# A retention, expert and rational-FFN kernel on one core: reordering the last stage's first steps, a drain, the y copies and the last two blocks

## The chip, the cores and the metric

The kernel runs on one core of a Trainium2 chip. The metric is the device time of one execution in microseconds (us). The engines have queues of their own and run in program order, each instruction waiting on semaphores for what it needs: TensorE (PE; its weight loads PEld overlap its matmuls), VectorE (DVE), ScalarE (ACT), GpSimd (POOL) and SyncE (SP), which issues most of the DMAs.

## The reference

Three stages follow one another. The change lies in the third, and touches the end of the second.

```python
# 1: a linear recurrence per head gives 1536 rows of 512 (B*S = 1536, D = 512)
state = gamma * state + k_t v_t^T;   y_t = scale * q_t @ state
# 2: each row goes to its best of 8 experts
h = relu(disp @ w1);   y = h @ w2;   x[i] = gate_w[i] * y[expert_idx[i], pos[i]]
# 3: a feed-forward layer with a rational function between two products
h = x @ w_in                                  # 512 -> 2048
P = a[0] + a[1] * h + a[2] * h*h + a[3] * h*h*h
Q = 1.0 + abs(b[0]) * abs(h) + abs(b[1]) * h*h
out = (P / (Q + 1e-06)) @ w_out               # 2048 -> 512
```

## The kernel before

The order of the work on each engine is the order in which the code issues it; no scheduler moves anything. Every product is made of three matmuls: an operand is split into a rounded part and the rest (`hi`, `lo`), and hi*hi, hi*lo and lo*hi are added up in a PSUM bank.

**The end of stage two.** Expert e has 256 rows in two tiles m = 0, 1. Its second product ends in two banks, which ScalarE copies out with the gate as scale (`y`, line 885); POOL then scatters the 128 rows of `y` to the DRAM table `yd` (line 787). The rows lie there sorted by expert, so the last two of the twelve tiles of 128 rows, 10 and 11, are loaded (`y_load`, `yr<-yd`) behind the scatters of the last expert. `y_tile` (lines 952 to 967) transposes a tile on TensorE into a bank (`ytp`) and splits it: ScalarE writes `yh`, VectorE `yl`.

**Stage three.** Four tiles of rows are one group `tb` of 512 rows (three groups), and the 2048 hidden columns are 16 chunks of 128. A chunk for one group is a *block*; there are 48, n = 0 to 47, and `ffn_at` gives each its quarter q of the weights, its group and its chunk f. Four blocks in a row add into the same four output banks `o` (one for each tile of the group), which are then drained into `acc`. The steps of a block:

- `ffn_a`: 12 matmuls give h (128 x 512) in a bank of its own (`l1`; four banks in turn, so block n+4 takes the bank of block n).
- `ffn_i`: three ScalarE passes (x, |h| and w; lines 995 to 997).
- `ffn_p`: two VectorE passes on x (lines 1004, 1005), and a POOL product for Q (line 1006).
- `ffn_r`: Ln and Exp on ScalarE (lines 1011, 1012); the result is 1/Q, written over h in its bank.
- `ffn_e`: three VectorE passes (lines 1017 to 1019): a Newton step, and P/Q into x. After them the bank of h is free.
- `ffn_g`: ScalarE rounds x to `gh` (line 1029), POOL makes the rest `gl` (line 1031; VectorE for the last two blocks).
- `ffn_b`: 12 matmuls, three for each tile m, add to the banks `o[m]`.

Step n of `ffn_step` issues a(n) and the later steps of older blocks: r(n-2), e(n-3), g(n-4), b(n-5) (`LAG`). Steps 0 to 3 stand between the last expert's second product, steps 4 to 52 in the loop of `ffn`. The eight banks are in four kinds (`BANKS`): `tp` (0, 1) takes transposes and the outputs o[0], o[1]; `l2` (2, 3) takes the experts' second product, the transposes of tiles 10 and 11, and o[2], o[3]; `l1` (4 to 7) takes h.

The first drain is that of block 3, in step 8 (`early`): before the change it is issued ahead of e(5) and p(7). Block 46 has no `ffn_b` of its own; block 47 does both. A finished tile of the output is scattered by POOL (`put_out`, line 1079).

Of the kernel before, what the change touches and what calls it, by code (L numbers as in the profile page):

```python
# [34 lines left out]
NA = 48  # L35
# [38 lines left out]
class Build:  # L74
# [742 lines left out]
    def moe(self):  # L817
        nc = self.nc
        with ExitStack() as st:
            self.dp = self.pool("dec", stack=st)  # L820
            self.mp = self.pool("moe", stack=st)
            self.outs = {}
            self.el, self.gx, self.gg, self.acc, self.pair = {}, {}, {}, {}, {}
            mp = self.mp
            self.xh, self.xl = {}, {}
            self.first_expert()
            for e in range(1, E):
# [4 lines left out]
                for fp in range(4):  # L832
                    i = 4 * e + fp // 2
                    wh, wl = self.whi[i], self.wlo[i]
                    ps = self.bank("l1").rearrange("p (a n) -> p a n", a=2)
# [27 lines left out]
                for hf in range(2):  # L863
                    i = 4 * e + 2 + hf
                    wh, wl = self.whi[i], self.wlo[i]
                    for m in range(2):
                        ms = slice(m * 128, m * 128 + 128)
                        for fl in range(4):
                            f = hf * 4 + fl
                            fh, fo = hh[f // 2][:, f % 2, ms], hl[f // 2][:, f % 2, ms]  # L870
                            ws = slice(fl * 512, fl * 512 + 512)
# [126 lines left out]
        self.el[n] = (x, w, h2, h)  # L998

    def ffn_p(self, n):  # L1000
        nc = self.nc
        ab = self.ab
        x, w, h2, h = self.el[n]
        nc.vector.tensor_tensor(out=x, in0=x, in1=h, op=ALU.mult)
        nc.vector.scalar_tensor_tensor(out=x, in0=x, scalar=ab[:, 1:2], in1=h, op0=ALU.add, op1=ALU.mult)
        nc.gpsimd.tensor_tensor(out=w, in0=h2, in1=w, op=ALU.mult)  # L1006
# [30 lines left out]
    def ffn_b(self, n):  # L1037
        first = n % 4 == 0 and (n == 0 or self.ffn_at(n - 1)[1] != self.ffn_at(n)[1])
        if first:
            self.ob = self.out_banks()  # L1040
        if n == 46:
            return
        ns = (46, 47) if n == 47 else (n,)
        gs = [self.gg.pop(k) for k in ns]
        for m in range(4):
            ps = self.ob[m]
            ms = slice(m * 128, m * 128 + 128)
            for k, (gh, gl) in zip(ns, gs):
                q, tb, f = self.ffn_at(k)
                last = f == 3 and (k == 47 or self.ffn_at(k + 1)[1] != tb)  # L1050
                wh, wl = self.whi[33 + 2 * q], self.wlo[33 + 2 * q]
                ws = slice(f * 512, f * 512 + 512)
                self.nc.tensor.matmul(ps, lhsT=gh[:, ms], rhs=wh[:, ws], start=first, stop=False)  # L1053
                self.nc.tensor.matmul(ps, lhsT=gh[:, ms], rhs=wl[:, ws], start=False, stop=False)  # L1054
                self.nc.tensor.matmul(ps, lhsT=gl[:, ms], rhs=wh[:, ws], start=False, stop=last)  # L1055
            if last:
                self.ffn_out(n, q, tb * 4 + m, ps)

# [30 lines left out]
    def ffn(self):  # L1089
        with ExitStack() as st:  # L1090
# [3 lines left out]
            for n in range(4, NA + LAG[3]):  # L1094
                self.ffn_step(n)

    def ffn_step(self, n):
        lr, le, lg, lb = LAG
        if n < NA:
            self.ffn_a(n)  # L1100
        if 0 <= n - lg < NA:
            self.ffn_g(n - lg)
        if 0 <= n - lr < NA:
            self.ffn_r(n - lr)
        if n < NA:
            self.ffn_i(n)
        early = n == lb + 3
        if early:
            self.ffn_b(n - lb)
        if 0 <= n - le < NA:  # L1110
            self.ffn_e(n - le)
        if 0 <= n - 1 < NA:
            self.ffn_p(n - 1)
        if n == 4:
            self.y_tile(8, self.bank("tp", "ytp"))
            self.y_tile(9, self.bank("tp", "ytp"))
        if n == 5:
            self.y_tile(10, self.bank("l2", "ytp"))
            self.y_tile(11, self.bank("l2", "ytp"))
        if n >= lb and not early:  # L1120
            self.ffn_b(n - lb)
            for t in self.outs.pop(n - 1, ()):
                self.put_out(t)
        if n in LOAD_AT:
            self.load_w(*LOAD_AT[n])
        for k in DEC_AT.get(n, ()):
            self.dec_act(k)
            self.dec_direct(k)
        for i, h in SPLIT_AT.get(n, ()):
            self.split_w(i, h)  # L1130
# [108 lines left out]
```

## Time and profile before

| | |
|---|---|
| time, median of 3 runs (lowest to highest) | 563.97 us (561.2 to 570.03) |
| the profiled execution: time | 562.63 us |
| its span, first to last instruction | 560.9 us |
| TensorE's mean granted clock | 0.994 of full |
| TensorE busy | 542.4 us, 97% of the span |
| DVE, ACT, POOL busy | 408.9, 391.2, 277.3 us |

The time of an execution is its span and some 1.7 us around it. In the tables of the trace, times are microseconds from the start of the span; an arrow names what ended the idle time of the engine ahead of an instruction.

### The profile page before, as it was taken

Reading aid. Unit: us, or ns where it says so; the run is one execution under the profiler, and the core shown is the slowest. Engines: PE = TensorE matmul, PEld = TensorE weight load, DVE = VectorE, ACT = ScalarE, POOL = GpSimd, SP = SyncE. Lnnn points to the kernel's source line nnn. Section 1 sums busy time; section 2 is a strip of 40 time slices with the busy share of each in tenths; the row PEclk is TensorE's granted clock in tenths of the full one; section 3 lists DMA queues with packets and bytes.
Section 4 is the critical chain, followed back from the end, with each engine's and each line's share of the span. In section 5 each row is a group of like instructions: output and inputs, shape, how many; then the busy total and the mean of one; then the engine's idle time right before and its main releaser. Section 6 shows DMA issues by size and latency. Waiting matters only on the chain.

```text
span 560.9 us, 9964 instructions
## 1 busy us (share of the span) xinstructions
PE 542.4 (97%) x3755; PEld 454.0 (81%) x3755; DVE 408.9 (73%) x627; ACT 391.2 (70%) x609; POOL 277.3 (49%) x212
## 2 busy tenths in 40 slices
PE   8999999999999999999997899999999999999994
PEld 4888887897898988989886788878787888888882
DVE  3537757576967768687548387889898999865972
ACT  2677853765666756666586789899979997766750
POOL 5545312308557373222053354667656766545673
PEclk9999999999999999999998999999999999999998
DMA  8689745497799999995323000222222200000212
GB/s 292 250 310 350 247 153 187 143 348 252 248 306 396 291 336 261 374 348 200 113 98 121 1 0 1 76 76 75 76 70 79 78 0 2 0 1 1 77 44 106
DMA packets 31171, 89.54 MB, mean 160 GB/s; under 512 B 6350, under 2 KB 6606, under 8 KB 31120
## 3 DMA queue, kind: packets, MB, share of 16 engines
q1 hardware_dynamic: 27216, 78.38, 41.8%
q0 software_dynamic: 3904, 10.50, 5.2%
q8 instruction: 30, 0.49, 0.4%
q14 instruction: 21, 0.17, 0.1%
HBM read 75.22 MB, written 14.69 MB: 160 GB/s over the span
## 4 chain that ended last, share of the span: by engine, by line
PE 64%; ACT 4%; DVE 3%; issue 2%; POOL 2%; POOLq 0%; ACTq 0%; DVEq 0%
PE h L982 7%; PE h L984 7%; PE h L983 7%; PE o L1053 6%; PE o L1055 6%; PE o L1054 6%; PE l L840 4%; PE l L842 4%; PE l L841 4%; PE l L874 4%; PE l L873 4%; PE l L872 4%; DVE wlo L137 1%; POOL out L1079 1%; PE tp L810 1%
## 5 line engine op out<-in xcount | busy, mean ns | idle before, releaser
L137 DVE TENSOR_TENSOR wlo<-raw,whi 128x1024 fp32r<-128x1024 f32 x80 | 107.6, 1354 | 25.6 <-ACT whi L131 24.8
L1031 POOL TENSOR_TENSOR gg<-fx,gg 128x512 fp32r<-128x512 f32 x46 | 65.8, 1432 | 69.6 <-issue 54.4
L131 ACT ACTIVATE whi<-raw 128x1024 fp32r<-128x1024 f32 x80 | 83.7, 1054 | 4.2 <-PE l L874 4.0
L1053 PE MATMUL o<-whi,gg 128*128 128x512 f32 x192 | 75.8, 395 | 4.0 <-DVE yl L965 3.1
L982 PE MATMUL h<-yh,whi 128*128 128x512 f32 x192 | 76.6, 399 | 2.4 <-DVE fx L1019 2.4
L984 PE MATMUL h<-yh,wlo 128*128 128x512 f32 x192 | 75.7, 394 | 0.0
L1055 PE MATMUL o<-whi,gg 128*128 128x512 f32 x192 | 75.5, 393 | 0.0
L983 PE MATMUL h<-yl,whi 128*128 128x512 f32 x192 | 75.5, 393 | 0.0
L1054 PE MATMUL o<-wlo,gg 128*128 128x512 f32 x192 | 74.9, 390 | 0.0
L995 ACT ACTIVATE fx<-h,ab 128x512 f32<-128x512 f32 x48 | 37.3, 777 | 47.2 <-PE h L984 47.1
L1006 POOL TENSOR_TENSOR fw<-fh,fw 128x512 f32<-128x512 f32 x48 | 62.4, 1299 | 9.7 <-ACT fw L997 9.6
L840 PE MATMUL l<-xh,whi 128*128 128x256 f32 x224 | 63.6, 284 | 1.1 <-DVEq L895 1.1
L842 PE MATMUL l<-xh,wlo 128*128 128x256 f32 x224 | 62.6, 279 | 0.0
L841 PE MATMUL l<-xl,whi 128*128 128x256 f32 x224 | 62.5, 279 | 0.0
L193 POOL TENSOR_TENSOR dw<-gq 128x512 int32<-128x512 int32 x16 | 23.1, 1443 | 62.1 <-DVE gq L190 33.6
L1053 PEld LDWEIGHTS o<-whi,gg 128*128 128x128 f32 x192 | 36.0, 188 | 12.7 <-DVE yl L965 3.8
L982 PEld LDWEIGHTS h<-yh,whi 128*128 128x128 f32 x192 | 36.5, 190 | 11.9 <-DVE fx L1019 4.1
L872 PE MATMUL l<-whi,hh 128*128 128x512 f32 x112 | 45.0, 402 | 0.0
L874 PE MATMUL l<-whi,hl 128*128 128x512 f32 x112 | 44.2, 395 | 0.0
L873 PE MATMUL l<-wlo,hh 128*128 128x512 f32 x112 | 44.2, 394 | 0.0
L1017 DVE SCALAR_TENSOR_TENSOR fw<-fw,cq,h 128x512 f32<-128x512 f32 x48 | 35.6, 741 | 11.4 <-ACT h L1012 11.4
L840 PEld LDWEIGHTS l<-xh,whi 128*128 128x128 f32 x224 | 42.0, 188 | 1.8 <-ACT y L885 1.6
(163 smaller groups left out, 1295.7 us busy)
## 6 DMA issues: line engine op xcount, KB each, us to landing
raw<-wm SPq DMA_DIRECT2D x64, 512.0 KB
r<-wf SPq DMA_DIRECT2D x32, 512.0 KB
vq<-vq SPq DMA_DIRECT2D x11, 512.0 KB
kk<-kk SPq DMA_DIRECT2D x11, 512.0 KB
wd<-dw SPq DMA_DIRECT2D x16, 256.0 KB
raw<-wd SPq DMA_DIRECT2D x8, 512.0 KB
xd<-xs SPq DMA_DIRECT2D x12, 256.0 KB
yr<-yd SPq DMA_DIRECT2D x12, 256.0 KB
```

The lines of the kernel that those rows point to most:

```text
L131: nc.scalar.activation(out=self.whi[i][:, sl], in_=raw, func=AF.Copy)
L137: nc.vector.tensor_tensor(out=self.wlo[i][:, sl], in0=raw, in1=self.whi[i][:, sl].bitcast(F32), op=ALU.subtract)
L840: nc.tensor.matmul(ps[:, fi], lhsT=wh[:, sl], rhs=xh[:, k], start=(k == 0), stop=False)
L841: nc.tensor.matmul(ps[:, fi], lhsT=wh[:, sl], rhs=xl[:, k], start=False, stop=False)
L842: nc.tensor.matmul(ps[:, fi], lhsT=wl[:, sl], rhs=xh[:, k], start=False, stop=(k == 3))
L872: nc.tensor.matmul(acc[m], lhsT=fh, rhs=wh[:, ws], start=(f == 0), stop=False)
L982: nc.tensor.matmul(h, lhsT=wh[:, sl], rhs=yh[:, k], start=(k == 0), stop=False)
L983: nc.tensor.matmul(h, lhsT=wh[:, sl], rhs=yl[:, k], start=False, stop=False)
L984: nc.tensor.matmul(h, lhsT=wl[:, sl], rhs=yh[:, k], start=False, stop=(k == 3))
L1053: self.nc.tensor.matmul(ps, lhsT=gh[:, ms], rhs=wh[:, ws], start=first, stop=False)
L1054: self.nc.tensor.matmul(ps, lhsT=gh[:, ms], rhs=wl[:, ws], start=False, stop=False)
L1055: self.nc.tensor.matmul(ps, lhsT=gl[:, ms], rhs=wh[:, ws], start=False, stop=last)
```

## The change

In steps 0 to 4, a flag `soon` issues g, r and e of a block one step earlier, p at the head of the step, and r behind i rather than ahead of it. The y copies of tiles 8 to 11 stand ahead of ffn_i in steps 4 and 5, no more behind ffn_p. The drain of block 3 in step 8 stands at the end of the step, behind e(5) and p(7), as in every other step. The matmuls of blocks 46 and 47 are interleaved by another list.

```diff
 def ffn_b(self, n):
...
-        ns = (46, 47) if n == 47 else (n,)
-        gs = [self.gg.pop(k) for k in ns]
-        for m in range(4):
-            ps = self.ob[m]
-            ms = slice(m * 128, m * 128 + 128)
-            for k, (gh, gl) in zip(ns, gs):
...
+        order = [(n, m) for m in range(4)]
+        if n == 47:
+            order = [(46, 0), (46, 1), (47, 0), (46, 2), (47, 1), (46, 3), (47, 2), (47, 3)]
+        gs = {k: self.gg.pop(k) for k in sorted({k for k, _ in order})}
+        for k, m in order:
...
+    def ffn_do(self, kind):
+        step, ns = self.todo[kind]
+        for n in ns:
+            step(n)
+
     def ffn_step(self, n):
         lr, le, lg, lb = LAG
+        soon = 1 if n < 5 else 0
+        for kind, lag, step in (("g", lg, self.ffn_g), ("r", lr, self.ffn_r), ("e", le, self.ffn_e)):
+            hi = min(NA, n - lag + soon + 1)
+            self.todo[kind] = (step, range(self.upto.get(kind, 0), hi))
+            self.upto[kind] = max(hi, self.upto.get(kind, 0))
         if n < NA:
             self.ffn_a(n)
-        if 0 <= n - lg < NA:
-            self.ffn_g(n - lg)
-        if 0 <= n - lr < NA:
-            self.ffn_r(n - lr)
+        if soon:
+            self.ffn_p(n - 1)
+        self.ffn_do("g")
+        if not soon:
+            self.ffn_do("r")
+        for t in {4: (8, 9), 5: (10, 11)}.get(n, ()):
+            self.y_tile(t, self.bank("tp" if n == 4 else "l2", "ytp"))
         if n < NA:
             self.ffn_i(n)
-        early = n == lb + 3
-        if early:
-            self.ffn_b(n - lb)
-        if 0 <= n - le < NA:
-            self.ffn_e(n - le)
-        if 0 <= n - 1 < NA:
+        if soon:
+            self.ffn_do("r")
+        self.ffn_do("e")
+        if not soon:
             self.ffn_p(n - 1)
-        if n == 4:
-            self.y_tile(8, self.bank("tp", "ytp"))
-            self.y_tile(9, self.bank("tp", "ytp"))
-        if n == 5:
-            self.y_tile(10, self.bank("l2", "ytp"))
-            self.y_tile(11, self.bank("l2", "ytp"))
-        if n >= lb and not early:
+        if n >= lb:
             self.ffn_b(n - lb)
```

The number and kind of the instructions are the same on every engine. POOL and SP keep their order, and TensorE's differs only in the last 24 matmuls.

ScalarE in steps 4 and 5, before (`fx`, the first `fh` and `fw` are i; the second `fh` and `h` are r; `yh` x2 are the copies of two tiles):

```order
L964 ACTIVATE yh_3875<-ytp 128x4x128 x2
L1029 ACTIVATE gg<-fx 128x512
L1011 ACTIVATE fh<-fw,cq 128x512
L1012 ACTIVATE h<-fh 128x512
L995 ACTIVATE fx<-h,ab 128x512
L996 ACTIVATE fh<-h 128x512
L997 ACTIVATE fw<-fh,b0a,b1a 128x512
L964 ACTIVATE yh_3875<-ytp 128x4x128 x2
```

and now:

```order
L1032 ACTIVATE gg<-fx 128x512
L965 ACTIVATE yh_3872<-ytp 128x4x128 x2
L996 ACTIVATE fx<-h,ab 128x512
L997 ACTIVATE fh<-h 128x512
L998 ACTIVATE fw<-fh,b0a,b1a 128x512
L1014 ACTIVATE fh<-fw,cq 128x512
L1015 ACTIVATE h<-fh 128x512
L965 ACTIVATE yh_3872<-ytp 128x4x128 x2
```

Ahead of the copies of tiles 10 and 11 (the second `yh`) stand, counted from the first pair: before, g(1), r(3) and i(5); now i(4) and r(3). In steps 1 and 2, r(0) and r(1) now also stand ahead of the last expert's two `y`, no more behind them.

VectorE in steps 8 and 9, before (`COPY` are the drains of o[0] and o[1] of block 3; `fw`, `h`, `fx` in a row are an e, two `fx` a p):

```order
L1067 COPY acc_4059<-o 128x512
L1067 COPY acc_4064<-o 128x512
L1017 SCALAR_TENSOR_TENSOR fw<-fw,cq,h 128x512
L1018 SCALAR_TENSOR_TENSOR h<-fx,ab,h 128x512
L1019 SCALAR_TENSOR_TENSOR fx<-fw,h 128x512
L1004 TENSOR_TENSOR fx<-fx,h 128x512
L1005 SCALAR_TENSOR_TENSOR fx<-fx,ab,h 128x512
```

and now:

```order
L1020 SCALAR_TENSOR_TENSOR fw<-fw,cq,h 128x512
L1021 SCALAR_TENSOR_TENSOR h<-fx,ab,h 128x512
L1022 SCALAR_TENSOR_TENSOR fx<-fw,h 128x512
L1007 TENSOR_TENSOR fx<-fx,h 128x512
L1008 SCALAR_TENSOR_TENSOR fx<-fx,ab,h 128x512
L1070 COPY acc_4065<-o 128x512
L1070 COPY acc_4070<-o 128x512
```

The five passes of e(5) and p(7) have moved ahead of the two copies.

TensorE in step 52, before (`o_5939` to `o_5942` are the banks of the four tiles; `gg_5967` is block 46, `gg_5985` block 47):

```order
L1053 MATMUL o_5939<-whi_5208,gg_5967 128x512
L1054 MATMUL o_5939<-wlo_5209,gg_5967 128x512
L1055 MATMUL o_5939<-whi_5208,gg_5967 128x512
L1053 MATMUL o_5939<-whi_5208,gg_5985 128x512
L1054 MATMUL o_5939<-wlo_5209,gg_5985 128x512
L1055 MATMUL o_5939<-whi_5208,gg_5985 128x512
L1053 MATMUL o_5940<-whi_5208,gg_5967 128x512
L1054 MATMUL o_5940<-wlo_5209,gg_5967 128x512
L1055 MATMUL o_5940<-whi_5208,gg_5967 128x512
L1053 MATMUL o_5940<-whi_5208,gg_5985 128x512
L1054 MATMUL o_5940<-wlo_5209,gg_5985 128x512
L1055 MATMUL o_5940<-whi_5208,gg_5985 128x512
```

and now:

```order
L1056 MATMUL o_5939<-whi_5208,gg_5967 128x512
L1057 MATMUL o_5939<-wlo_5209,gg_5967 128x512
L1058 MATMUL o_5939<-whi_5208,gg_5967 128x512
L1056 MATMUL o_5940<-whi_5208,gg_5967 128x512
L1057 MATMUL o_5940<-wlo_5209,gg_5967 128x512
L1058 MATMUL o_5940<-whi_5208,gg_5967 128x512
L1056 MATMUL o_5939<-whi_5208,gg_5985 128x512
L1057 MATMUL o_5939<-wlo_5209,gg_5985 128x512
L1058 MATMUL o_5939<-whi_5208,gg_5985 128x512
L1056 MATMUL o_5941<-whi_5208,gg_5967 128x512
L1057 MATMUL o_5941<-wlo_5209,gg_5967 128x512
L1058 MATMUL o_5941<-whi_5208,gg_5967 128x512
```

Block 46 now has two tiles ahead of the first matmul that reads block 47, no more one; the last three matmuls are those of block 47 for the fourth tile in both.

## Rows read from the trace of the kernel before

**Rows 1.** The page, part 1: busy us, share of the span, instructions.

```profile
PE 542.4 (97%) x3755; PEld 454.0 (81%) x3755; DVE 408.9 (73%) x627; ACT 391.2 (70%) x609; POOL 277.3 (49%) x212
```

**Rows 2.** TensorE's waits: engine, line, waited for: us in total, times, longest.

```profile
PE o L1053 <- DVE yl L965: 3.1, 1, 3.1
PE h L982 <- DVE fx L1019: 2.4, 4, 1.4
```

**Rows 3.** The timeline, steps 5 to 7: start us, us, engine, line, operation.

```profile
295.63 0.50 PE L1053 MATMUL o<-whi,gg 128*128 128x512 f32 x1
...
299.04 1.06 ACT L964 ACTIVATE yh<-ytp 128x512 fp32r<-128x512 f32 x2
...
300.39 0.50 PE L1053 MATMUL o<-whi,gg 128*128 128x512 f32 x1 [3.11 <-DVE yl L965]
...
306.23 0.39 PE L1053 MATMUL o<-whi,gg 128*128 128x512 f32 x1
...
308.97 0.39 PE L982 MATMUL h<-yh,whi 128*128 128x512 f32 x1
```

**Rows 4.** Two windows: us, TensorE busy (matmuls), granted clock, DMA share, GB/s.

```profile
303.00:304.00 1.00, 1.00 (x4) 0.50 0.00 0
...
319.00:323.00 4.00, 2.55 (x11) 1.00 0.00 0
```

**Rows 5.** The timeline of ScalarE, steps 3 to 5.

```profile
288.45 0.78 ACT L995 ACTIVATE fx<-h,ab 128x512 f32<-128x512 f32 x1 [0.83 <-PE h L984]
...
292.27 0.77 ACT L995 ACTIVATE fx<-h,ab 128x512 f32<-128x512 f32 x1
...
294.27 1.06 ACT L964 ACTIVATE yh<-ytp 128x512 fp32r<-128x512 f32 x2
...
295.75 0.72 ACT L1011 ACTIVATE fh<-fw,cq 128x512 f32<-128x512 f32 x1
...
297.04 0.76 ACT L995 ACTIVATE fx<-h,ab 128x512 f32<-128x512 f32 x1
```

**Rows 6.** The timeline, last expert's outputs, their scatter and the loads behind them.

```profile
280.09 0.69 ACT L885 ACTIVATE y<-l,tab 128x512 f32<-128x512 f32 x1 [0.68 <-PE l L874]
...
282.11 1.31 POOL L1006 TENSOR_TENSOR fw<-fh,fw 128x512 f32<-128x512 f32 x1
...
285.69 0.69 ACT L885 ACTIVATE y<-l,tab 128x512 f32<-128x512 f32 x1 [0.68 <-PE l L874]
...
289.34 0.80 SPq L949 DMA_DIRECT2D yr<-yd  x2
...
294.60 1.03 PE L962 MATMUL ytp<-ct,yr 128*128 128x128 f32 x8
```

**Rows 7.** The timeline, step 8 and the head of step 9.

```profile
318.07 1.38 DVE L1067 COPY acc<-o 128x512 f32<-128x512 f32 x2 [8.88 <-PE o L1055]
...
319.72 0.39 PE L1055 MATMUL o<-whi,gg 128*128 128x512 f32 x1
...
321.55 0.50 PE L982 MATMUL h<-yh,whi 128*128 128x512 f32 x1 [1.45 <-DVE fx L1019]
```

**Rows 8.** The timeline of the tail.

```profile
546.37 0.98 POOL L1079 DMA_INDIRECT out<-acc,perm  x1 [0.30 <-issue]
...
548.03 0.50 PE L1053 MATMUL o<-whi,gg 128*128 128x512 f32 x1 [0.93 <-ACT gg L1029]
...
548.76 0.50 PE L1055 MATMUL o<-whi,gg 128*128 128x512 f32 x1
...
553.04 0.98 POOL L1079 DMA_INDIRECT out<-acc,perm  x1 [0.40 <-DVE acc L1071]
553.43 0.69 DVE L1071 TENSOR_TENSOR acc<-o,acc 128x512 f32<-128x512 f32 x1 [0.67 <-PE o L1055]
554.40 0.98 POOL L1079 DMA_INDIRECT out<-acc,perm  x1 [0.38 <-DVE acc L1071]
```

**Rows 9.** The line of the expert scatters: durations in ns, min/median/max.

```profile
L787 POOL DMA_INDIRECT yd<-y,sidx x16: 982/1012/2034, 98.2 to 286.7; - x16
```

More of the change, by code (lines that the diff above doesn't have):

```diff
@@ L823, in moe @@
             self.el, self.gx, self.gg, self.acc, self.pair = {}, {}, {}, {}, {}
+            self.todo, self.upto = {}, {}
             mp = self.mp
@@ L1000, in ffn_p @@
     def ffn_p(self, n):
+        if not 0 <= n < NA:
+            return
         nc = self.nc
@@ L1042, in ffn_b @@
             return
-        ns = (46, 47) if n == 47 else (n,)
-        gs = [self.gg.pop(k) for k in ns]
-        for m in range(4):
-            ps = self.ob[m]
-            ms = slice(m * 128, m * 128 + 128)
-            for k, (gh, gl) in zip(ns, gs):
[L1049 to L1055, printed above, removed]
+        order = [(n, m) for m in range(4)]
[3 more added lines that the diff above has]
+        for k, m in order:
+            q, tb, f = self.ffn_at(k)
+            last = f == 3 and (k == 47 or self.ffn_at(k + 1)[1] != tb)
+            (gh, gl), ps, ms = gs[k], self.ob[m], slice(m * 128, m * 128 + 128)
+            wh, wl = self.whi[33 + 2 * q], self.wlo[33 + 2 * q]
+            ws = slice(f * 512, f * 512 + 512)
+            self.nc.tensor.matmul(ps, lhsT=gh[:, ms], rhs=wh[:, ws], start=first, stop=False)
+            self.nc.tensor.matmul(ps, lhsT=gh[:, ms], rhs=wl[:, ws], start=False, stop=False)
+            self.nc.tensor.matmul(ps, lhsT=gl[:, ms], rhs=wh[:, ws], start=False, stop=last)
             if last:
```

## The prediction

> **What bounds the kernel now.** I read the page's first part, then TensorE's waits, then the timeline around each wait. TensorE is busy for 97% of the span [rows 1], and its order of matmuls stays as it is up to the last 24. So only stalls of TensorE can be won or lost, and in stage three these are few [rows 2]: one of 3.1 us ahead of an o matmul, waiting for a `yl` copy, and four of 2.4 us together ahead of an h matmul, waiting for the last pass of an e; the longest of these is 1.45. A third stands in the tail. The change touches just these three places.
>
> The first is b(0) in step 5 [rows 3]. It starts at 295.63. Six matmuls go to o[0] and o[1]; the seventh, into o[2], needs the bank that holds the transposed tile 10 until VectorE has copied it. ScalarE begins the two copies at 299.04, VectorE follows, and the matmul runs at 300.39. A second loss stands behind the first: in 303 to 304 only 4 matmuls start and the granted clock is 0.50, 1.2 GHz instead of 2.4 [rows 4]. From 300.39 to b(1) at 306.23 there are 18 matmuls in 5.84 us; b(1) itself takes 2.74 for 12, 0.228 each [rows 3], so 18 cost 4.11 and 1.73 are lost to the clock.
>
> The second is a(9), which takes over the bank of block 5 [rows 7]. VectorE had been idle for 8.88 us when it began the drains at 318.07: they were issued ahead of e(5) and waited for b(3) while e(5), which needs nothing from b(3), stood behind them. The last matmul of b(3) starts at 319.72, a(9) at 321.55: 1.83, less 0.23 that follow anyway, is 1.60 lost.
>
> The third is the wait for block 47's `gg` at 548.03, and for its second half at 548.76 [rows 8].
>
> **The change, part by part.** *The copies ahead of the passes, and g, r, e a block sooner.* These two go together, since both set when ScalarE comes to tile 10. Costs from start to start on ScalarE [rows 5]: i takes 294.27 - 292.27 = 2.00; two copies and a g 295.75 - 294.27 = 1.48; an r 297.04 - 295.75 = 1.29. i(3) starts at 288.45, when TensorE ends h(3); I take that as fixed. From there the new order is i(3) 2.00, r(2) 1.29, g(1) with the copies of tiles 8 and 9 1.48, i(4) 2.00, r(3) 1.29: 8.06, so the copies of tiles 10 and 11 start at 296.51 instead of 299.04, 2.53 sooner. The transposes they read start at 294.60 [rows 6], which is early enough. VectorE has only e(2) between the two pairs; its r(2) ends at 288.45 + 3.29 = 291.74, so I count e(2) as done. With the same hops the seventh matmul moves from 300.39 to 297.86. Undisturbed it would be at 295.63 + 6 x 0.228 = 297.00, so 0.86 of waiting is left. That is nearer to the 1.45 us stall than to the 3.11 one, and around the 1.45 stall, in 319 to 323, the granted clock stays at 1.00 [rows 4]. I therefore take the dip as gone. b(1) then starts 18 x 0.228 after 297.86, at 301.97 instead of 306.23: **4.26 us won**, 2.53 of waiting and 1.73 of clock. The bounds: 2.53 if the clock dips all the same, 5.1 if the rest of the wait goes too (2.53 + 1.73 + 0.86).
>
> What this costs elsewhere. In steps 1 and 2 the r stands ahead of the last expert's `y` on ScalarE. The first `y` starts at 280.09 after 0.68 of idling [rows 6]; r(0) fills the idle time from 279.41 and ends at 280.70, so `y` is 0.61 late. Queued behind it on POOL are the scatter and then fw(1), whose product r(1) needs. `y` to fw took 282.11 - 280.09 = 2.02 and fw 1.31, so fw(1) ends at 284.03; ScalarE comes to r(1) at 285.01 (the second `y`, 285.69, less its 0.68 of idling). Covered by 1.0. One round later: second `y` at 286.30, fw(2) done at 289.63, r(2) due at 290.45: covered by 0.8. SP's queue: the loads of tiles 10 and 11 start at 289.34 and last 0.80, plus 0.61 is 290.75; TensorE transposes them at 294.60. Covered by 3.85. i(5) now waits for the second pair of copies, 297.57 instead of 297.04; its h bank is taken over only by a(9). Cost of all these: nothing, as long as those covers hold.
>
> *The first drain.* With e(5) and p(7) ahead, the copies still find their banks when b(3) ends, since VectorE has 8.88 us for five passes. Who waits next: b(4), which needs the drained banks only after a(9), 2.74 later. e(6) now stands behind the copies and starts near 319.45 instead of after 321.5, so it is not later than it was. **1.60 won.** The lower bound is 0 (a(9) waits for something else then), the upper 1.60.
>
> *The last two blocks.* The first matmul on block 47 still waits to 548.03, and its third to 548.76, because both come from ScalarE and VectorE. Now six matmuls of block 46 are done by then, no more three. But o[0], o[1] and o[2] still end 3, 9 and 15 matmuls after that wait, as before; only o[3] ends three matmuls, 0.68, sooner. Its drain would be over at 553.44 instead of 554.12. POOL's scatters, however, come one after another: that of o[2] runs from 553.04 to 554.02, and the least gap between two is 0.30 [rows 8], so the last starts at 554.32 instead of 554.40. **0.08 won**; bounds 0 and 0.68.
>
> The interleaving changes banks from one group of three matmuls to the next. b(1) does that in all its 12 matmuls, at 0.228 each [rows 3], with the engine at 97% [rows 1]. The Trainium skill, TensorE: Matmul & The Clock Gate, section "A second HAM failure mode: psum-queue depth-cycling", says that going through PSUM banks in turn leaves small idle times between groups, by which the clock swings between its levels. The trace does not agree: by the row this costs 0, by the rule it would be the fifth case below.
>
> The sum: 4.26 + 1.60 + 0.08 = 5.94. The profiled execution took 562.63, so 556.7 by it. The median of the runs is 1.34 above that execution, which would give 558.0. I forecast between the two, **557.3 us**; the case times below start from the same 563.3 less what is won.
>
> **The rivals.**
>
> 1. *The clock falls after the shorter stall too.* For it: the stall sits at the same place, right behind the stretch in which TensorE turned to transposes. Against: less than a third of the wait is left, and the 1.45 us stall brought no dip. 1.73 comes back: 559.1. Chance 0.13.
>
> 2. *The copies are not sooner.* ScalarE is then held by an r that waits for POOL: r(2) for fw(2), which has 0.8 of cover, r(3) behind it. If the chain slips by 2.53, stall and dip are as before and only the drain and the tail count: 561.6. For it: the order r, `y`, scatter, fw, r is a ring over two engines, and it was not one before. Against: the covers. Chance 0.09.
>
> 3. *That ring grows, and the kernel gets slower.* From the cover of 0.8 on, each us of the last expert's scatter holds r(2), and all behind it on ScalarE, for a us; TensorE waits at o[2]. 2.53 of slip uses up the shorter wait and brings the dip back; 1.68 more uses up drain and tail. So it decides at 0.8 + 2.53 + 1.68 = 5.0 over the usual 1.0 of a scatter. The longest in the trace took 2.03 [rows 9]. At 8 us it would give 565.3. Chance 0.03.
>
> 4. *More goes than counted.* The rest of the stall, 0.86, and the three other waits for e, 2.4 - 1.45 = 0.95 [rows 2], vanish when VectorE and ScalarE run ahead: 555.5. Nothing moves in those later steps, so chance 0.06.
>
> 5. *Bank changes slow the tail*, at half rate for its 24 matmuls: 24 x 0.228 = 5.5 lost, 562.8. Against: b(1). Chance 0.02.
>
> **How the numbers follow.** The forecast has 0.67. Its own bounds are 555.5 (case 4) and 559.1 (case 1); with cases 2 and 5 the upper end goes to 562. Three runs of the kernel before lay between 561.2 and 570.03, so a median can lie 1.4 off, as here. I take 554.2 to 562.5. A change under 2%, some 11 us, is about what a measurement of this kernel cannot tell from none, and all that can be won at the three places is 5.1 + 1.60 + 0.68 + 0.95 = 8.3: within 2% 0.94, faster 0.04, slower 0.02.
>
> **What would show it.** Right: TensorE's wait ahead of the seventh o matmul is near 0.9 instead of 3.1, with the first copy of tile 10 some 2.5 us sooner against h(3); no window at 0.50 behind it; no wait ahead of a(9), and VectorE's e(5) well ahead of the copies; a tail whose matmuls end 0.7 sooner while the last scatter moves by 0.1. Wrong: a wait of r on POOL in steps 1 to 4, transposes of tiles 10 and 11 that wait for their loads, or a new wait for e behind step 9, where the time won would be given back.

## The result, and the profile after

The changed kernel took 557.39 us (median of 4 runs, 556.43 to 557.99), the kernel before 563.71 (4 runs); the ratio is 0.9871, with a 95% interval of 0.983 to 0.9912. The forecast was 557.3 in a range of 554.2 to 562.5. The profiled execution took 556.43, its span is 554.7.

TensorE's waits in stage three, of the kernel after (us in total, times, longest), against [rows 2]:

```profile
PE h L983 <- DVE fx L1022: 1.0, 3, 0.4
...
PE o L1056 <- DVE yl L966: 0.9, 1, 0.9
...
PE o L1056 <- ACT gg L1032: 0.2, 1, 0.2
```

The wait for the `yl` copy is 0.9 instead of 3.1. Of the four waits for e the one of 1.45 is gone, and the other three stand as they were. The wait for block 47 is 0.2 instead of 0.9.

The timeline of the kernel after, steps 3 to 6, beside [rows 3, 5]: i(3), r(2), g(1), the first pair of copies, i(4), r(3), the second pair and VectorE behind it; last the seventh matmul of b(0), and b(1).

```profile
288.11 0.78 ACT L996 ACTIVATE fx<-h,ab 128x512 f32<-128x512 f32 x1 [1.07 <-PE h L985]
...
290.13 0.71 ACT L1014 ACTIVATE fh<-fw,cq 128x512 f32<-128x512 f32 x1
...
291.40 0.62 ACT L1032 ACTIVATE gg<-fx 128x512 fp32r<-128x512 f32 x1
...
291.93 1.07 ACT L965 ACTIVATE yh<-ytp 128x512 fp32r<-128x512 f32 x2
...
292.88 0.78 ACT L996 ACTIVATE fx<-h,ab 128x512 f32<-128x512 f32 x1
...
294.90 0.71 ACT L1014 ACTIVATE fh<-fw,cq 128x512 f32<-128x512 f32 x1
...
296.18 1.06 ACT L965 ACTIVATE yh<-ytp 128x512 fp32r<-128x512 f32 x2
...
296.79 1.29 DVE L966 TENSOR_TENSOR yl<-ytp,yh 128x512 fp32r<-128x512 f32 x2 [0.92 <-ACT yh L965]
...
297.54 0.50 PE L1056 MATMUL o<-whi,gg 128*128 128x512 f32 x1 [0.87 <-DVE yl L966]
...
301.77 0.39 PE L1056 MATMUL o<-whi,gg 128*128 128x512 f32 x1
```

ScalarE goes through the list without a gap: the copies of tiles 10 and 11 start 8.07 us after i(3); 8.06 were summed up. The wait left is 0.87; 0.86 were summed up. Two windows behind it, granted clock in the column after TensorE's busy time, beside [rows 4]:

```profile
298.00:301.00 3.00, 3.00 (x15) 1.00 0.28 115
301.00:305.00 4.00, 4.00 (x20) 1.00 0.00 0
```

The clock stays at 1.00, and 20 matmuls fall in the 4 us. In step 8, beside [rows 7]:

```profile
313.59 1.38 DVE L1070 COPY acc<-o 128x512 f32<-128x512 f32 x2 [3.41 <-PE o L1058]
...
315.46 0.40 PE L983 MATMUL h<-yh,whi 128*128 128x512 f32 x1
```

The drains found their banks when b(3) ended, and a(9) has no wait in front. The tail, beside [rows 8]:

```profile
541.93 0.50 PE L1056 MATMUL o<-whi,gg 128*128 128x512 f32 x1 [0.24 <-ACT gg L1032]
...
542.66 0.50 PE L1058 MATMUL o<-whi,gg 128*128 128x512 f32 x1
...
546.19 0.39 PE L1058 MATMUL o<-whi,gg 128*128 128x512 f32 x1
...
546.90 0.98 POOL L1082 DMA_INDIRECT out<-acc,perm  x1 [0.37 <-DVE acc L1074]
548.19 0.99 POOL L1082 DMA_INDIRECT out<-acc,perm  x1 [0.30 <-issue]
```

To compare all runs without what happens ahead of tile 8, I measure three stretches in the one trace of each run: from the first transpose of tile 8 to b(1), from there to a(9), and from there to the start of the last scatter. Before, these are 306.23 - 290.99 = 15.24, 321.55 - 306.23 = 15.32 and 554.40 - 321.55 = 232.85; after, 301.77 - 290.64 = 11.13, 315.46 - 301.77 = 13.69 and 548.19 - 315.46 = 232.73. So 4.11 + 1.63 + 0.12 = 5.86 us were won in them. The other 0.3 of the 6.2 between the two spans lies ahead of the first transpose of tile 8. The change moves work of ScalarE and VectorE there too (steps 0 to 3), but two traces of the changed kernel differ by more in that part: the transpose starts at 290.64 in one and at 292.05 in the other (after_again).

| kernel | median us | ratio (95%) | tile 8 to b(1) | to a(9) | to the last scatter |
|---|---|---|---|---|---|
| before | 563.71 | 1 | 15.24 | 15.32 | 232.85 |
| after | 557.39 | 0.9871 (0.983 to 0.9912) | 11.13 | 13.69 | 232.73 |
| after_again | 558.26 | 0.99 (0.9862 to 0.9939) | 11.12 | 13.69 | 232.68 |
| e1, drain | 562.56 | 0.9971 (0.9936 to 1.0005) | 14.95 | 13.69 | 232.76 |
| e2, steps and copies | 560.87 | 0.9951 (0.9913 to 0.9989) | 11.12 | 15.30 | 232.82 |
| e3, steps | 562.46 | 1.0001 (0.9967 to 1.0035) | 13.11 | 15.30 | 232.84 |
| e4, copies | 566.67 | 1.005 (1.0031 to 1.0069) | 18.31 | 15.30 | 232.85 |
| e9, copies taken apart | 560.79 | 0.9922 (0.9885 to 0.9959) | 11.66 | 15.30 | 232.81 |
| e5, tail | 564.63 | 0.9988 (0.9947 to 1.0028) | 15.24 | 15.30 | 232.81 |
| e8, block 46 first | 558.63 | 0.9914 (0.9881 to 0.9947) | 11.16 | 13.70 | 233.12 |
| e6, r(3) behind the copies | 558.57 | 0.9905 (0.9874 to 0.9936) | 10.14 | 13.69 | 232.69 |
| e7, and splits first | 555.68 | 0.9894 (0.9837 to 0.9951) | 10.12 | 13.69 | 231.04 |
| e7_again | 555.68 | 0.9854 (0.9809 to 0.9899) | 10.11 | 13.69 | 231.02 |
| e10, and a new tail | 554.66 | 0.981 (0.9777 to 0.9844) | 10.14 | 13.69 | 229.68 |

Each ratio is against runs of the kernel before on the same chip. Where no edit touches them the stretches repeat to 0.1 us, with one exception: the first stretch of e1 is 14.95 against 15.24, as the same wait of 3.11 is followed there by a clock loss of 1.44 instead of 1.73. The medians also carry what varies ahead of tile 8. Part of that can be seen: in the profiled executions of e2, e6, e8 and e9 the granted clock is also 0.50 for some 3 to 7 us near 55 us, in stage one, which no edit touches (last section). So small terms are read from the stretches.

### The profile page after: what moved, and what is told of

It is laid out like the page before. It is cut to its first block, busy times and chain, and to the rows that moved or that the text cites. A ratio compares the mean times of both kernels' runs of the same rounds, so it can differ in the third digit from the quotient of the medians.

```text
span 554.7 us, 9954 instructions
## 1 busy us (share of the span) xinstructions
PE 540.3 (97%) x3743; PEld 453.0 (82%) x3755; DVE 410.5 (74%) x627; ACT 391.0 (70%) x609; POOL 279.0 (50%) x212
## 4 chain that ended last, share of the span: by engine, by line
PE 65%; ACT 3%; DVE 3%; issue 2%; POOL 2%; POOLq 0%; ACTq 0%; DVEq 0%
PE h L983 7%; PE h L985 7%; PE h L984 7%; PE o L1056 6%; PE o L1058 6%; PE o L1057 6%; PE l L841 4%; PE l L843 4%; PE l L873 4%; PE l L875 4%; PE l L842 4%; PE l L874 4%; DVE wlo L137 1%; POOL out L1082 1%; PE tp L810 1%
## 5 line engine op out<-in xcount | busy, mean ns | idle before, releaser
L1056 PEld LDWEIGHTS o<-whi,gg 128*128 128x128 f32 x192 | 36.0, 188 | 9.4 <-DVE yl L966 1.3
L1058 PEld LDWEIGHTS o<-whi,gg 128*128 128x128 f32 x192 | 36.0, 188 | 8.7 <-DVE gg L1034 0.4
```

## The experiments

**The changed kernel once more (after_again).**

> The changed kernel once more, to stand beside the three that are built on it on the same chip. Theory: 6 us less than the kernel before, ratio 0.9893 by the prediction's sum, as in the first measurement (0.9871, 0.983 to 0.9912); the wait at o[2] in step 5 is 0.9 and there is no window at half clock behind it in this profile too. Rival: the dip behind the shorter wait comes in some executions; then the ratio is 0.992 or the profile shows it.

The wait at o[2] is 0.89 here, the stretches are those of the first trace, and no matmul behind the wait is slow. The ratio, 0.99, holds the sum.

**The drain alone (e1).**

```diff
-        early = n == lb + 3
-        if early:
-            self.ffn_b(n - lb)
...
-        if n >= lb and not early:
+        if n >= lb:
```

> The kernel before with one edit: the drain of block 3 stands at the end of step 8, behind e(5) and p(7). My theory: TensorE's wait ahead of a(9), 1.45 us, goes whole and nothing takes its place; all else stays as before (wait of 3.1 at o[2] in step 5, clock dip behind it). 1.6 us less than before, ratio 0.997. Rival: the drain's copies, now behind p(7), come late to the banks of b(4), and the time is the same as before.

The second stretch is 13.69, 1.63 less than before and the same as in the changed kernel, and nothing is later in the third. The ratio agrees, though its interval just holds 1.

**The steps and the copies without drain and tail (e2).**

```diff
+        early = n == lb + 3
+        if early:
+            self.ffn_b(n - lb)
         self.ffn_do("e")
```

> The changed kernel with the early drain and the old tail put back, so only the steps a block sooner and the copies ahead of the passes are left. My theory: TensorE waits 0.9 at o[2] in step 5, no window at half clock, b(1) starts 4.1 to 4.3 us sooner against h(3) than before; the wait ahead of a(9) is 1.45 as before: 4.2 us less than before, ratio 0.9925. Rival (gains not additive, since blocks that run ahead hide the drain too): the wait ahead of a(9) is gone here as well, and 5.8 us are won.

First stretch 11.12 as in the changed kernel, second 15.30: the wait of 1.45 ahead of a(9) is there whole. The gains add; blocks that run ahead do not hide the drain, which was the rival.

**The steps alone (e3), and the copies alone (e4).** In e3 the two `y_tile` lines go back to the end of the step. In e4 they are all that moves:

```diff
+        for t in {4: (8, 9), 5: (10, 11)}.get(n, ()):
+            self.y_tile(t, self.bank("tp" if n == 4 else "l2", "ytp"))
         if n < NA:
             self.ffn_i(n)
```

> As e2, but the copies of tiles 8 to 11 stand at the end of steps 4 and 5 as before: only the steps are a block sooner. From the costs on ScalarE the second pair of copies starts some 0.5 us sooner than before, and the first pair 1.3 later than before, so b(0) itself starts about 1 us late and then waits 2 us at o[2]. My theory (the copies' place is what counts): 0.5 us won if the clock dips behind these two waits, 2.3 if it does not. Rival (the sooner steps are what counts): 4 us won, as in e2.

> The kernel before with one edit: the copies of tiles 8 to 11 stand ahead of ffn_i in steps 4 and 5; no step is sooner. On ScalarE i(3), g(0), r(2), two copies, i(4), g(1), r(3) stand ahead of the copies of tiles 10 and 11: 8.6 us after h(3), against 10.6 before and 8.1 in the changed kernel. My theory: the wait at o[2] is 1.4 us instead of 3.1 and the clock keeps its full rate: 3.7 us won, ratio 0.9934. Rival: the clock dips at this length of wait too: 2.0 us won. Second rival (the steps are what counts): under 1 us won.

In e3, two waits come as summed up. The timeline, and a window behind them:

```profile
297.86 0.50 PE L1056 MATMUL o<-whi,gg 128*128 128x512 f32 x1 [1.27 <-DVE yl L966]
...
300.84 0.50 PE L1056 MATMUL o<-whi,gg 128*128 128x512 f32 x1 [1.31 <-DVE yl L966]
```

```profile
301.00:305.00 4.00, 4.00 (x18) 1.00 0.03 11
```

They are 1.27 and 1.31 long, 2.58 in sum against the 3.11 of before, but the clock does not dip behind them. So 15.24 - 13.11 = 2.13 us are won in this execution. Of these 1.63 are clock (from the seventh matmul of b(0) to b(1) it takes 305.05 - 300.84 = 4.21, before 5.84), and the other 0.50 is waiting. The timed ratio, 1.0001, does not show that: 2.13 is 0.9962, just outside its interval. The mean granted clock over a whole run is 0.996 to 0.998 in ten of its 12 runs, and 0.994 or less in 25 of 31 of the kernel before, so the dip seems gone in most of them; as that mean covers the whole span, this is not shown. Why the timing shows less than the trace stays open; what varies ahead of tile 8 is some us, as large as what is looked for.

e4 refutes my expectation. It is slower than before. The timeline shows a wait that I had not seen coming:

```profile
294.92 1.03 PE L962 MATMUL ytp<-ct,yr 128*128 128x128 f32 x8
...
296.19 1.07 ACT L964 ACTIVATE yh<-ytp 128x512 fp32r<-128x512 f32 x2
...
296.80 1.29 DVE L965 TENSOR_TENSOR yl<-ytp,yh 128x512 fp32r<-128x512 f32 x2 [7.22 <-ACT yh L964]
...
298.01 0.73 DVE L1017 SCALAR_TENSOR_TENSOR fw<-fw,cq,h 128x512 f32<-128x512 f32 x1
...
299.44 0.69 DVE L1019 SCALAR_TENSOR_TENSOR fx<-fw,h 128x512 f32<-128x512 f32 x1
...
300.19 0.80 PE L982 MATMUL h<-yh,whi 128*128 128x512 f32 x1 [4.24 <-DVE fx L1019]
```

a(5) waits 4.24 us for the last pass of e(1), whose bank it takes. r(1) had ended near 291.5, but e(1) stood behind the two `yl` copies on VectorE, which idled 7.22 us for transposes that TensorE makes only after a(4). And the clock falls:

```profile
301.00:305.00 4.00, 4.00 (x10) 0.50 0.44 179
```

Only ten matmuls fall in these 4 us, at 0.50. Moving `y_tile` ahead of i moves its VectorE half ahead of e as well. In the changed kernel this does no harm, since e(1) is issued a step sooner and is over by then.

**The copies taken apart (e9).** This tells whether it is the VectorE half.

```diff
         nc.scalar.activation(out=self.yh[tb][:, :, sl], in_=tp, func=AF.Copy)
-        nc.vector.tensor_tensor(
...
+        if t < 8:
+            self.y_rest(t, tp)
+        else:
+            self.ylate[t] = tp
...
             self.ffn_e(n - le)
+        for t in {4: (8, 9), 5: (10, 11)}.get(n, ()):
+            self.y_rest(t, self.ylate.pop(t))
```

> As e4 (copies ahead of ffn_i, no step sooner), but the copies are taken apart: ScalarE's yh stays ahead of ffn_i, VectorE's yl stands behind ffn_e and ahead of ffn_p. My theory of why e4 lost: its yl copies stood ahead of e(1) and e(2) on VectorE, so a(5) waited 4.2 us for e(1), which waited behind the copies for transposes that follow a(4). Here that chain is cut: a(5) does not wait, o[2] waits 1.4 us at full clock, and 3.7 us are won against the kernel before, ratio 0.9934. Rival (in e4 it was ScalarE's copies that held r and so e): a(5) still waits over 2 us and the kernel is no faster than before.

a(5) does not wait, and the one wait at o[2] is the 1.4 of the sum:

```profile
304.35 0.50 PE L1061 MATMUL o<-whi,gg 128*128 128x512 f32 x1 [1.39 <-DVE yl L973]
```

```profile
305.00:309.00 4.00, 4.00 (x19) 1.00 0.04 16
```

15.24 - 11.66 = 3.58 are won, with full clock behind the wait, and the ratio agrees. So the place of ScalarE's copies alone carries 3.58 of the 4.11; that steps are sooner adds 0.5 directly, and lets the copies move in one piece.

**The tail alone (e5), and all of block 46 first (e8).** e5 is the kernel before with the new list; e8 is the changed kernel with this one:

```diff
-            order = [(46, 0), (46, 1), (47, 0), (46, 2), (47, 1), (46, 3), (47, 2), (47, 3)]
+            order = [(k, m) for k in (46, 47) for m in range(4)]
```

> The kernel before with one edit: the list of the last two blocks is the interleaved one. Theory (POOL's scatters bound the tail): TensorE's wait for block 47 shrinks from 0.9 to 0.25 and its last matmul starts 0.7 us sooner against the end of b(45), the last scatter starts 0.1 sooner: nothing that timing can tell, ratio 1.000. Rival: TensorE's end sets the tail, 0.7 us less.

> The changed kernel with another list for the last two blocks: all four tiles of block 46, then all four of block 47. TensorE never waits for block 47 then and ends some 0.8 us sooner than in the changed kernel. Theory (the tail is bound by POOL's scatters, one each 1.29 us from the first on): the first tile ends 0.7 later, so do all scatters, and the last one starts 0.5 us later against the end of b(45), 0.5 slower. Rival (TensorE's end sets the tail): 0.8 faster.

TensorE's last matmul starts 231.46 us after a(9) before (553.01), 230.81 in e5, 230.73 after, and 229.90 in e8. The last scatter starts after 232.85, 232.81, 232.73 and 233.12. So TensorE ends 0.83 sooner in e8 than in the changed kernel, and the kernel's last scatter comes 0.39 later. POOL's scatters in e8:

```profile
551.88 0.98 POOL L1082 DMA_INDIRECT out<-acc,perm  x1 [3.48 <-DVE acc L1074]
553.17 0.98 POOL L1082 DMA_INDIRECT out<-acc,perm  x1 [0.30 <-DVE acc L1074]
554.46 0.98 POOL L1082 DMA_INDIRECT out<-acc,perm  x1 [0.30 <-issue]
555.75 0.98 POOL L1082 DMA_INDIRECT out<-acc,perm  x1 [0.31 <-issue]
```

They follow one another at 1.29 with the least gap of 0.30, so here POOL spaces them, and the first sets the last. In the kernel before that is not so: its four are 1.36 to 1.39 apart, each gap (0.38 to 0.41) ends with VectorE's addition of that tile, and TensorE's six matmuls a tile, 6 x 0.228 = 1.37, set the pace. In the changed kernel only the last scatter comes at the least gap. The timed ratios could not tell e5 or e8 from its neighbour.

**What is left of the wait at o[2] (e6).**

```diff
-            hi = min(NA, n - lag + soon + 1)
+            hi = min(NA, n - lag + (soon and (n < 4 or kind != "r")) + 1)
...
-        if not soon:
+        if n > 5:
             self.ffn_do("r")
         for t in {4: (8, 9), 5: (10, 11)}.get(n, ()):
             self.y_tile(t, self.bank("tp" if n == 4 else "l2", "ytp"))
+        if n == 5:
+            self.ffn_do("r")
```

> The changed kernel with one edit: r(3) stands behind the copies of tiles 10 and 11 instead of ahead of them (step 5, ahead of i(5)). Theory (ScalarE's chain is what the o matmul in step 5 waits for): the copies start 1.0 us sooner, at the end of i(4), the wait of 0.9 at o[2] goes whole and b(1) starts 1.0 sooner against h(3); nothing waits for r(3), whose bank is taken over by a(7). 1.0 us less than the changed kernel. Rival: the transposes or VectorE's e(2) hold the copies, and the wait stays at 0.4 or more.

The wait is gone, and the first stretch is 10.14, 0.98 less than in after_again. Timing on the same chip, 0.9905 against 0.99, does not resolve it.

**The three later waits (e7, e7_again).** The two loops at the end of `ffn_step` change places:

```diff
+        for i, h in SPLIT_AT.get(n, ()):
+            self.split_w(i, h)
         for k in DEC_AT.get(n, ()):
             self.dec_act(k)
             self.dec_direct(k)
-        for i, h in SPLIT_AT.get(n, ()):
-            self.split_w(i, h)
```

> As e6, and in the steps that hold a weight split and a decode (16, 18, 21, 27, 29, 31) the split stands ahead of the decode. In the changed kernel's trace the three waits for e that are left (0.4, 0.2, 0.4 us, with the restarts 1.5) stand behind a VectorE subtraction that takes 2.2 us instead of 1.25 while POOL adds. Theory: ahead of the decode the subtraction runs beside no POOL addition and takes 1.25, and the three waits go: 1.5 less than e6, 2.5 less than the changed kernel, ratio to before 0.983 to 0.985. Rival: the order only moves the collision to another VectorE pass, and the waits stay within 0.2 of what they were.

> The kernel of e7 once more, since its interval was wide (0.9837 to 0.9951). By its trace, 0.98 of the wait at o[2] and the three later waits with their restarts, 1.47, are gone against the changed kernel: 8.3 us less than the kernel before, ratio 0.9853. Rival: the later part of stage three gives it back in other executions, and the ratio is that of the changed kernel, 0.99.

The changed kernel ahead of the first of these waits, POOL's addition, VectorE's subtraction and the h matmul behind e:

```profile
361.19 1.30 POOL L193 TENSOR_TENSOR raw<-gq 128x512 int32<-128x512 int32 x1 [1.75 <-ACT gq L182]
...
361.34 2.23 DVE L137 TENSOR_TENSOR wlo<-raw,whi 128x1024 fp32r<-128x1024 f32 x1 [0.29 <-ACT whi L131]
...
365.67 0.50 PE L983 MATMUL h<-yh,whi 128*128 128x512 f32 x1 [0.43 <-DVE fx L1022]
```

The same subtraction in e7, ahead of the decode:

```profile
359.49 1.23 DVE L137 TENSOR_TENSOR wlo<-raw,whi 128x1024 fp32r<-128x1024 f32 x1 [1.31 <-ACT whi L131]
```

1.23 instead of 2.23, and the three waits are gone: the third stretch is 1.65 shorter than in e6, where 1.47 had been summed up; the difference was not taken apart. The first timing, 0.9894, missed the 0.983 to 0.985 expected, with a wide interval that just reaches it; the second, 0.9854, is the ratio summed up.

**The tail at its cause (e10).**

```diff
+        if n == 46:
+            self.late = (gl, x, gh)
+            return
...
         self.ffn_do("e")
+        if n == 50:
+            gl, x, gh = self.late
+            self.nc.vector.tensor_tensor(out=gl, in0=x, in1=gh.bitcast(F32), op=ALU.subtract)
...
-            order = [(46, 0), (46, 1), (47, 0), (46, 2), (47, 1), (46, 3), (47, 2), (47, 3)]
+            order = [(k, m) for m in range(4) for k in (46, 47)]
```

> The kernel of e7 with the tail changed at its cause: the rest of block 46 (gl, VectorE) stands behind e(47) instead of ahead of it, and the two last blocks are taken tile by tile as in the kernel before. VectorE then goes from e(46) to e(47) without the idle 0.76 and the 0.69 of the subtraction in between. Theory (the first of the four last scatters, and through it block 47's chain on VectorE, sets the end): block 47 is there 1.3 us sooner, TensorE waits for it under 0.2, the first scatter starts 1.3 sooner against the end of b(45), and so does the last. 1.3 us less than e7. Rival: the scatters, one each 1.36 us, or TensorE's wait for the rest of block 46 keep the end where it was, within 0.4.

The rests of blocks 46 and 47 on VectorE, and the first and the last of the four scatters:

```profile
539.50 0.68 DVE L1133 TENSOR_TENSOR gg<-fx,gg 128x512 fp32r<-128x512 f32 x1
...
540.34 0.69 DVE L1038 TENSOR_TENSOR gg<-fx,gg 128x512 fp32r<-128x512 f32 x1 [0.16 <-ACT gg L1032]
...
542.60 0.98 POOL L1085 DMA_INDIRECT out<-acc,perm  x1 [1.55 <-DVE acc L1077]
...
546.71 0.98 POOL L1085 DMA_INDIRECT out<-acc,perm  x1 [0.38 <-DVE acc L1077]
```

TensorE does not wait in the tail any more, and the last scatter starts 229.68 after a(9), 1.36 sooner than in e7 (the first is 1.42 sooner). The four are 1.36 to 1.39 apart as in the kernel before, at the pace of six matmuls a tile, so it is the sooner start on block 47 that is won, and not a closer row of scatters. The late rest and the list were not tried one by one. At 0.981 of the time before this version has the lowest median; its interval (0.9777 to 0.9844) overlaps that of e7_again.

## Why the prediction was right

*The seventh matmul of b(0).* The sum said 297.86 - 288.45 = 9.41 us after i(3); it came after 297.54 - 288.11 = 9.43. The chain on ScalarE is what it waited for: e6 shortened just that chain, and the rest of the wait went. The 18 matmuls behind it took 301.77 - 297.54 = 4.23 instead of 4.11, so the gain is some 0.15 below the 4.26 forecast.

*The clock.* I took the dip as gone because the 0.86 left was nearer to a wait without a dip. That held in both traces of the changed kernel, and in e3 (two waits of 1.3) and e9 (1.39). With the wait of 3.11 (before) and of 4.24 (e4) the granted clock fell to 0.50. The first case did not come. The length of a wait is no safe measure, though: in stage one the clock fell behind a wait of 2.02 (e2) and not behind one of 2.67 (e4), as the last section shows. The 0.87 is shorter than every wait named here, so the guess was a good one, but not a certain one.

*The covers.* r(1) and r(2) stood behind the scatters on POOL with 1.0 and 0.8 to spare. In the trace r(2) starts at 290.13, 2.02 after i(3), as soon as ScalarE is free. Cases 2 and 3 did not come.

*The drain.* 1.60 forecast, 1.63 in e1 and in the changed kernel, with nothing late behind it.

*The tail.* 0.08 forecast, 0.12 measured, 0.04 in e5; differences so small are within what the stretches vary. What is shown is that TensorE's ending 0.7 sooner is not won. The reason given holds: the last scatter of the changed kernel comes at the least gap, 0.30, behind the third, and in e8, where TensorE ends sooner still, all four are spaced by POOL.

*The other waits for e* (case 4) did not shrink by themselves, 0.43, 0.20 and 0.37, and it took e7 to remove them. *Bank changes* (case 5) did not slow the tail. A window in it, with the interleaved blocks:

```profile
540.00:546.00 6.00, 5.75 (x25) 1.00 0.27 107
```

The granted clock is 1.00. The section of the Trainium skill that the prediction weighed, "A second HAM failure mode: psum-queue depth-cycling" in TensorE: Matmul & The Clock Gate, tells of swings of the clock in another, bf16, kernel that went through its banks in turn. The trace does not show them, as forecast.

*What the prediction left out.* It put the copies and the sooner steps together as "both set when ScalarE comes to tile 10". e4 shows that there is a second reason: without the sooner e, the copies on VectorE hold a(5). The sum did not suffer, as it counted e(2) as done and e(1) was; but the same way of counting, ScalarE alone, gave the wrong sign for e4.

*The numbers.* That the first two terms are right to 0.15 us is no accident, since each has an experiment of its own. That the median came within 0.1 of 557.3 is luck: that figure was set between 556.7 and 558.0, and the same kernel gave 558.26 in after_again. The prediction also held that a change under 2% can hardly be told from none here; the interval, 0.983 to 0.9912, leaves out 1, so 1.3% could be told.

## What to carry to other kernels

When a step is moved, follow it on every engine that it issues to: the half on the engine one did not look at can hold work that was ready, and turn a gain of 3.6 us into a loss of 3. An instruction that waits for the newest result belongs behind those whose inputs are already there (the drain, the `yl` copies, the rest of block 46). In a tail, find out what spaces the last outputs: TensorE's six matmuls a tile in the kernel before and in e10, POOL's scatters in e8, where TensorE's ending 0.83 sooner won nothing. What won time was to have the first output early (e10).

## What the runs showed of the hardware

In stage three the granted clock fell to 0.50 with waits of TensorE of 3.11 and 4.24 us, and stayed at 1.00 behind 1.45, 1.39, 0.87, and two of 1.3 with 1.7 us of matmuls between. The wait of 3.11 cost 1.73 us beyond its own length (1.44 in e1). That of 4.24 cost 2.7: a(5) and the transposes behind it took 306.51 - 300.19 = 6.32 in e4, and the same work 298.87 - 295.26 = 3.61 in e6. To break the long wait in two (e3) already saved this in the profiled execution.

The length of the wait alone does not decide. In stage one, which no edit touches, a matmul of one line of the code (L278, the same in all) came late in several traces. In e2, with a window behind it:

```profile
53.20 0.24 PE L278 MATMUL sc<-vq,kk 64*64 64x64 f32 x1 [2.02 <-issue]
```

```profile
55.00:59.00 4.00, 4.00 (x22) 0.50 0.53 211
```

and in e4:

```profile
54.47 0.24 PE L278 MATMUL sc<-vq,kk 64*64 64x64 f32 x1 [2.67 <-issue]
```

```profile
55.00:59.00 4.00, 4.00 (x72) 1.00 0.67 268
```

The shorter wait was followed by a clock of 0.50, the longer one by 1.00. In e6, e8 and e9 (2.26, 3.36 and 3.27) it was 0.50 again. What else decides stays open here.

A VectorE subtraction of two SBUF tiles took 2.23 us where POOL added at the same time, and 1.23 where it did not; ahead of the other two waits that e7 removed it took 2.09 and 2.22. In the rows of the changed kernel (under e7) it starts at 361.34, while POOL's addition runs to 362.49, and ends 1.08 after that one. POOL's next pass, the subtraction of ffn_g, in turn takes 2.30; the same pass takes 1.30 at 291.17 in the kernel before:

```profile
362.44 2.30 POOL L1034 TENSOR_TENSOR gg<-fx,gg 128x512 fp32r<-128x512 f32 x1
```

The Trainium skill, SBUF — State Buffer, section "Who interferes with whom", says that VectorE and GpSimd share a pair of ports that one instruction holds alone, so that the other waits for its end. The trace agrees: each of the two that came second took a us more, and the first, 1.30, none.
